# The first run-time branch of phase 2 moved ahead of the preparation of the first expert rows

## The chip, the core and the metric

The kernel runs on one core of one Trainium2 chip. A core has five engines, each with its own stream of instructions that it works off in order: TensorE (PE, matmuls), VectorE (DVE), ScalarE (ACT), GpSimd (POOL) and SyncE (SP). SP, ACT and POOL also start transfers (DMAs). Engines wait for each other by semaphores. The metric is device time in microseconds (us) for one execution.

## The reference, cut to what matters

Three stages follow one another: banded attention with 32 global tokens (4 batches, 8 heads, 512 + 32 positions, head size 64), a channel mix of width 1024, and a mixture of 8 experts, of which each of the 2176 rows uses one. Phase 2 of the kernel is the last loop of this:

```python
for b in range(B):
    prev_e = -1
    for s in range(S):
        fresh_e = int(np.argmax(logits[b, s]))
        e = fresh_e if s == 0 or local_gate[b, s] < 0.5 or prev_e < 0 else prev_e
        prev_e = e
        p = softmax(logits[b, s])
        h = np.maximum(x[b, s] @ w1[e], 0.0)      # 512 -> 1024
        out[b, s] = p[e] * (h @ w2[e])            # 1024 -> 512
```

How many rows an expert gets is known only on the chip.

## The kernel before

**Phase 1** does attention, the channel mix and the routing. A planner (`Sched`) sets its order. It leaves in HBM the mixed rows `y`, and in SBUF a list `idx` of the rows of each expert and a count `cint` of the 128-row pieces that each expert has. One piece of expert 0 is worked off already inside phase 1 (`ahead`, from L788); its result tile `oa` is sent to the output by an indirect DMA on POOL at L844.

**Phase 2** (`Experts.run`, L944) is written out by hand, and every engine works off its instructions in the order of the text. For each expert e in turn it branches on the count `cs[e]` (`first`, L932): two pieces or more go through `full` (L867, matmuls of 256 columns, tile `ph`), one piece goes through `tail` (L884, rows as the stationary operand, tile `pht`), and none leaves only the preparation of what comes next. All three sides hold the same side work, handed in as lists: `W` (conversions of the next weights) and `X` (the rows of the next expert).

**Rows.** `gather` (L852) fetches one or two pieces from `y` into a tile `xs` by indirect DMAs on POOL (L856). `prep` (L857) turns half of them: four transposes on PE into `pt` (L863), then ACT writes the high part `xh` (L865) and DVE the low part `xl` (L866). PE's first matmul of an expert needs `xh`, its third `xl`.

**Weights.** They come in parts of 512 KB into staging tiles, `st` (three, in use since phase 1) and `sw` (two, new in phase 2, in the memory that phase 1's tiles held, `oa`'s group among them). ACT makes the high part (`slot..h`, L776), DVE or POOL the low part (L779). `fetch` (L761) starts as many loads as staging tiles are free. Nearly all loads are issued by SP. Only the first two into `sw` are issued by ACT: `s.fetch(s.nc.scalar)` at L954 (the DMA itself has line L767).

**The seam between the phases** reads, in the order of the text: gathers of expert 0 (L948), reading the counts into registers of each engine (L949), `prep` of expert 0's first rows in two halves (L952), the gather for expert 1 (L953), ACT's two loads (L954), and then the loop with its first branch (L936, and L940 on the side where it is not two pieces). Each engine reads the counts and branches for itself.

The program prints both branch sides of `first` and its caller below. In the profiled execution expert 0 and expert 1 go through `tail`.

## Time and profile before

| | us |
|---|---|
| median of 3 runs (lowest, highest) | 812.99 (810.97, 813.35) |
| the profiled execution, its own time | 810.05 |
| its span | 808.3 |
| PE busy | 744.3 (92% of the span) |
| DVE, ACT, POOL busy | 523.0, 398.0, 368.3 |

The profiled execution lies 2.94 us under the median of the runs. PE is the busy engine nearly everywhere; the place of the change is one of the few where it stands still. Phase 2 begins at about 537 us of the span. Times in rows are us from the start of the span unless a column says ns; "idle before" in square brackets is how long the engine had nothing to do, and after the arrow what ended it ("issue": nothing that the profile shows as work of another).

### The profile page before, as it was taken

How to read it: one execution, taken by the hardware profiler on the slowest of the kernel's cores; microseconds unless marked ns; L12 is line 12 of the kernel's file. 1: busy time of each engine (PE TensorE's matmuls, PEld its weight loads, DVE VectorE, ACT ScalarE, POOL GpSimd, SP SyncE). 2: the span in 40 equal slices, each digit the busy share in tenths (PEclk: the TensorE clock that was granted, in tenths of full speed). 3: DMA queues.
4: the chain of work that ended last, by engine and by line, in shares of the span. 5: the costliest groups of instructions: out<-in, count | busy, mean ns of one | idle time of the engine just before them, and what ended most of it. 6: DMA issues, size and time to landing. Idle time of an engine off the chain costs nothing.

```text
span 808.3 us, 14249 instructions
## 1 busy us (share of the span) xinstructions
PE 744.3 (92%) x4790; PEld 626.2 (77%) x4790; DVE 523.0 (65%) x1482; ACT 398.0 (49%) x985; POOL 368.3 (46%) x495
## 2 busy tenths in 40 slices
PE   5987899899999999899998999987899999999974
PEld 3655687698878878888887897766697999998963
DVE  6699889776695775785766845765672725435431
ACT  4796676563555754655644432416461615224420
POOL 6678868745255462554471422134552513324130
PEclk9997899999999999899999899997999999999988
DMA  6674242211112102112102300428873523517210
GB/s 151 162 188 138 80 113 64 72 27 41 37 28 75 43 12 72 37 29 62 24 3 102 105 27 14 141 55 253 267 269 142 193 99 129 180 65 249 84 56 7
DMA packets 93966, 78.71 MB, mean 97 GB/s; under 512 B 70559, under 2 KB 74655, under 8 KB 93859
## 3 DMA queue, kind: packets, MB, share of 16 engines
q1 hardware_dynamic: 89202, 63.23, 26.2%
q0 software_dynamic: 4240, 13.11, 5.0%
q8 instruction: 54, 0.88, 0.4%
q10 hardware_dynamic: 416, 1.05, 0.4%
q14 instruction: 54, 0.43, 0.2%
HBM read 68.44 MB, written 9.70 MB: 97 GB/s over the span
## 4 chain that ended last, share of the span: by engine, by line
PE 66%; DVE 14%; DMA 10%; issue 3%; POOL 3%; ACT 2%; SPq 0%; POOLq 0%; ACTq 0%; DVEq 0%
DMA xs<-y,idx 6%; PE av L236 4%; PE psk L21 4%; PE psk L23 4%; PE psk L24 4%; PE psv L21 4%; PE psv L24 4%; PE psv L23 3%; PE ptp L228 3%; PE ph L23 3%; PE ph L24 3%; PE ph L21 3%; PE po L21 3%; PE po L23 3%; PE po L24 3%
## 5 line engine op out<-in xcount | busy, mean ns | idle before, releaser
L222 POOL TENSOR_SCALAR pl<-pl,mx 128x192 f32<-128x192 f32 (+1 forms) x128 | 66.3, 529 | 73.0 <-DVE mx L219 45.1
L21 PE MATMUL psk<-xs,slot0h 128*128 128x256 f32 x256 | 75.6, 301 | 0.9 <-ACT xs L448 0.8
L216 ACT ACTIVATE pl<-pl,mx 128x224 f32<-128x224 f32 (+1 forms) x128 | 58.8, 461 | 35.3 <-DVE mx L213 29.8
L23 PE MATMUL psk<-xs,slot0h 128*128 128x256 f32 x256 | 74.9, 293 | 0.0
L24 PE MATMUL psk<-xs,slot0l 128*128 128x256 f32 x256 | 74.9, 293 | 0.0
L856 POOL DMA_INDIRECT xs<-y,idx x32 | 38.4, 1201 | 64.3 <-PE pt L863 39.5
L922 POOL DMA_INDIRECT out_dram<-osb,idx x19 | 23.5, 1238 | 96.3 <-DVE osb L921 82.3
L450 POOL TENSOR_TENSOR xs<-xm,xs 128x512 fp32r<-128x512 f32 (+1 forms) x36 | 46.4, 1297 | 44.7 <-ACT xs L448 44.7
L877 ACT ACTIVATE hh<-ph 128x256 fp32r<-128x256 f32 x56 | 21.5, 384 | 84.1 <-PE ph L24 82.8
L443 POOL TENSOR_SCALAR xm<-xT,mut 128x256 f32<-128x256 f32 (+7 forms) x96 | 43.3, 466 | 29.6 <-DVE xT L294 16.2
L21 PE MATMUL psv<-slot1h,kh 128*128 128x512 f32 x136 | 55.0, 406 | 0.0
L23 PE MATMUL psv<-slot1l,kh 128*128 128x512 f32 x136 | 54.4, 401 | 0.3 <-POOL slot1l L417 0.3
L24 PE MATMUL psv<-slot1h,kl 128*128 128x512 f32 x136 | 54.2, 401 | 0.0
L21 PEld LDWEIGHTS psk<-xs,slot0h 128*128 128x128 f32 x256 | 49.7, 196 | 2.2 <-ACT xs L448 1.2
L23 PEld LDWEIGHTS psk<-xs,slot0h 128*128 128x128 f32 x256 | 50.5, 197 | 0.8 <-issue 0.2
L24 PEld LDWEIGHTS psk<-xs,slot0l 128*128 128x128 f32 x256 | 50.3, 197 | 0.5
L228 PE MATMUL ptp<-ident,pl 128*128 128x128 f32 x256 | 43.3, 288 | 7.6 <-DVE mxg L269 1.5
L236 PE MATMUL av<-ph,v 128*128 128x256 f32 x192 | 44.5, 292 | 2.3 <-DVE xT L294 1.0
L119 DVE TENSOR_TENSOR plo<-ptp,ph 128x512 fp32r<-128x512 f32 x48 | 32.7, 685 | 19.0 <-ACT ph L117 18.7
L878 DVE SCALAR_TENSOR_TENSOR hl<-ph,hh 128x256 fp32r<-128x256 f32 x56 | 23.7, 423 | 32.9 <-ACT hh L877 32.5
L446 DVE SCALAR_TENSOR_TENSOR xm<-xT,mut,xm 128x256 f32<-128x256 f32 (+7 forms) x96 | 41.2, 466 | 3.6 <-POOL xm L443 3.4
L228 PEld LDWEIGHTS ptp<-ident,pl 128*128 128x128 f32 x256 | 30.2, 145 | 14.7 <-POOL pl L222 4.3
(730 smaller groups left out, 2497.6 us busy)
## 6 DMA issues: line engine op xcount, KB each, us to landing
st<-in_moe_w_dram SPq DMA_DIRECT2D x42, 512.0 KB, 4.3
sw<-in_moe_w_dram SPq DMA_DIRECT2D x20, 512.0 KB, 4.4
y<-r SPq DMA_DIRECT2D x17, 256.0 KB, 2.0
qn<-in_q_l_dram SPq DMA_DIRECT2D x32, 128.0 KB, 3.0
kn<-in_k_l_dram SPq DMA_DIRECT2D x32, 128.0 KB, 2.9
earlyh<-in_moe_w_k_dram SPq DMA_DIRECT2D x8, 512.0 KB, 5.0
raw<-in_moe_w_v_dram SPq DMA_DIRECT2D x8, 512.0 KB, 3.6
vn<-in_v_l_dram SPq DMA_DIRECT2D x24, 96.0 KB, 2.1
```

What stands on the lines that cost most here:

```text
L21: i=nc.tensor.matmul(out,wh,xh,start=first,stop=False)
L23: nc.tensor.matmul(out,wh,xl,start=False,stop=False)
L24: return nc.tensor.matmul(out,wl,xh,start=False,stop=last)
L119: nc.vector.tensor_sub(out[1],x,out[0].bitcast(F32))
L216: nc.scalar.activation(p[:,h,ks],p[:,h,ks],AF.Exp,bias=mx[:,h:h+1],scale=-1.0,accum_out=mx[:,4+h:5+h])
L222: nc.gpsimd.tensor_scalar(out=p[:,h,ks],in0=p[:,h,ks],scalar1=mx[:,6+h:7+h],scalar2=0.0,op0=ALU.mult,op1=ALU.add)
L228: nc.tensor.transpose(pt[:,c,h],p[:,h,c*96:c*96+P],s.ident)
L236: nc.tensor.matmul(o,s.v(u,x,i,c),P_[y][:,c],start=c==m==0,stop=c==1 and m==len(parts)-1)
L443: nc.gpsimd.tensor_scalar(out=x[:,u,o:o+k],in0=s.xT[b][:,c,q:q+k],scalar1=m[:,1,c:c+1],scalar2=0.0,op0=ALU.mult,op1=ALU.add)
L446: nc.vector.scalar_tensor_tensor(out=x[:,u,o:o+k],in0=s.xT[b][:,c,1+q:1+q+k],scalar=m[:,0,c:c+1],in1=x[:,u,o:o+k],op0=ALU.mult,op1=ALU.add)
L450: nc.gpsimd.tensor_sub(xl[:,cs,:n],x[:,:,:n],xh[:,cs,:n].bitcast(F32))
L856: s.nc.gpsimd.indirect_dma_start(out=s.xs[i][:,j,:],out_offset=None,in_=s.y,in_offset=IndirectOffsetOnAxis(ap=s.idx[:,ch:ch+1],axis=0))
```

## The change

The two halves of `prep` and the gather for expert 1 no longer stand ahead of the loop. They become a list `rows`, handed to `first` for expert 0 alone, and run as the first thing inside the sides: all three where there are two pieces or one, and only the gather where there is none. ACT's two loads (`s.fetch(s.nc.scalar)`) stay where they were, ahead of the loop.

```diff
-    def first(s,i,i2,e,c,W,own,X):
+    def first(s,i,i2,e,c,W,own,X,rows=()):
...
         with tc.If(c>=2) as two:
-            s.full(i,e,0,list(W),[*own,*X])
+            [g() for g in rows]; s.full(i,e,0,list(W),[*own,*X])
             s.more(i2,e,1,c)
         with two.Else():
-            with tc.If(c==1) as one: again(); s.tail(i,e,0,list(W),list(X))
+            with tc.If(c==1) as one: again(); [g() for g in rows]; s.tail(i,e,0,list(W),list(X))
             with one.Else():
                 again()
-                for g in (*W,*X): g()
+                for g in (*rows[2:],*W,*X): g()
...
-        for hf in range(2): s.prep(at(0,0),0,hf)
-        s.gather(1,0)
         s.fetch(s.nc.scalar)
...
+        rows=[lambda: s.prep(at(0,0),0,0),lambda: s.prep(at(0,0),0,1),lambda: s.gather(1,0)]
         for e in range(E):
-            s.first(at(e,0),at(e,1),e,cs[e],[s.whole]*(8 if e else min(8,16-LN)) if e+1<E else (),own(e),others(e))
+            s.first(at(e,0),at(e,1),e,cs[e],[s.whole]*(8 if e else min(8,16-LN)) if e+1<E else (),own(e),others(e),() if e else rows)
```

On PE, at the seam, the order of instructions from before (minus) to the change (plus); `xs_5870` are expert 0's rows, `ph` is the first tile of the side with two pieces:

```order
 L949 TENSOR_LOAD cint
 L949 TENSOR_LOAD cmax
+L936 COMPARE_AND_BRANCH
 L863 MATMUL pt<-ident,xs_5870 128x128 x8
-L936 COMPARE_AND_BRANCH
 L21 MATMUL ph<-xh_7296,slot2h 128x256
```

The branch now stands in front of the eight transposes.

On ACT at the same place; `sw` are the two staging tiles that ACT itself loads, `xh_7296` is the high part of expert 0's rows:

```order
 L949 TENSOR_LOAD cint
 L949 TENSOR_LOAD cmax
-L865 ACTIVATE xh_7296<-pt 128x512 x2
 L767 DMA sw_7304<-in_moe_w_dram 128x1024
 L767 DMA sw_7305<-in_moe_w_dram 128x2x512
 L936 COMPARE_AND_BRANCH
+L865 ACTIVATE xh_7296<-pt 128x512 x2
 L877 ACTIVATE hh<-ph 128x256 x2
```

The two evictions have gone behind the branch, and behind the two loads too.

On ACT at the head of the side with one piece (behind L940), where `slot1h` are conversions of expert 1's weights:

```order
 L929 UNCONDITIONAL_BRANCH
 L940 COMPARE_AND_BRANCH
+L865 ACTIVATE xh_7296<-pt 128x512 x2
 L776 ACTIVATE slot1h<-st_5869 128x1024
 L776 ACTIVATE slot1h<-st_5867 128x1024
```

The evictions stand there in front of the conversions.

## Rows read from the trace of the kernel before

**Rows 1.** The page: span, and one group of DMA issues.
```profile
span 808.3 us, 14249 instructions
...
out_dram<-osb,idx POOLq DMA_INDIRECT x19, 3.6
```
**Rows 2.** Busy time of each engine (instructions), PE's granted clock, DMA share, in a stretch.
```profile
core 0: us, PE busy (x) PEld busy (x) DVE busy (x) ACT busy (x) POOL busy (x), PEclk, DMA share, GB/s
600.00:700.00 100.00, 98.88 (x615) 88.63 (x614) 49.46 (x62) 37.11 (x61) 36.38 (x25) 1.00 0.47 164
```
**Rows 3.** PE in order of time: start, us, engine, line, tiles, [idle before].
```profile
540.48 0.34 PE L681 MATMUL psL<-rt,A 128*128 128x136 f32 x2
540.87 0.30 PE L863 MATMUL pt<-ident,xs 128*128 128x128 f32 x1
542.93 0.98 PE L863 MATMUL pt<-ident,xs 128*128 128x128 f32 x7 [1.76 <-DMA xs<-y,idx]
548.74 0.77 PE L21 MATMUL pht<-slot2h,xh 128*128 128x512 f32 x1 [4.82 <-issue]
...
558.20 0.60 PE L863 MATMUL pt<-ident,xs 128*128 128x128 f32 x4
...
568.30 0.77 PE L21 MATMUL pht<-slot1h,xh 128*128 128x512 f32 x1 [3.79 <-issue]
```
**Rows 4.** ACT in order of time, its DMA issues (ACTq) among it.
```profile
543.58 1.08 ACT L865 ACTIVATE xh<-pt 128x512 fp32r<-128x512 f32 x2 [9.55 <-PE pt L863]
548.52 2.17 ACTq L767 DMA_DIRECT2D sw<-in_moe_w_dram  x2
551.03 2.95 ACT L776 ACTIVATE slot1h<-st 128x1024 fp32r<-128x1024 f32 x3 [6.37 <-issue]
...
575.05 0.60 ACT L906 ACTIVATE hs<-pht 128x512 f32<-128x512 f32 x1 [4.12 <-DMA out_dram<-osb,idx]
```
**Rows 5.** The line L844, the DMA of `oa`: issue, who waited, landing.
```profile
L844 POOL DMA_INDIRECT out_dram<-oa,idx x1: 1032/1032/1032, 542.5 to 542.5; - x1
...
  ACT slot1h L776: 6.4, 1
...
DMA to landing us min/median/max: 5.9/5.9/5.9
```
**Rows 6.** The line L767, 540 to 560 us: ns min/median/max, first and last start.
```profile
L767 ACTq EVENT_SEMAPHORE  x3: 17/38/38, 544.0 to 548.4; - x3
L767 ACTq DMA_DIRECT2D sw<-in_moe_w_dram x2: 393/1068/1743, 548.5 to 548.9; - x2
L767 SPq DMA_DIRECT2D sw<-in_moe_w_dram x2: 340/340/341, 558.3 to 559.4; - x2
```
**Rows 7.** POOL in order of time, 537 to 560 us.
```profile
542.49 1.03 POOL L844 DMA_INDIRECT out_dram<-oa,idx  x1 [0.30 <-issue]
544.08 0.98 POOL L856 DMA_INDIRECT xs<-y,idx  x1 [0.56 <-PE pt L863]
555.86 2.41 POOL L779 TENSOR_TENSOR slot1l<-sw,slot1h 128x1024 fp32r<-128x1024 f32 x1 [9.55 <-ACT slot1h L776]
```
**Rows 8.** All gathers (line L856): issue to landing.
```profile
DMA to landing us min/median/max: 3.3/5.0/7.8
```
**Rows 9.** The chain that ended last, in order of time, 535 to 552 us.
```profile
543.58 0.60 ACT xh L865
544.21 0.58 DVE xl L866
...
545.51 3.23 issue
```
**Rows 10.** Busy time by stretch again (columns as above), after PE's two longest stops.
```profile
548.74:554.62 5.88, 5.88 (x14) 4.63 (x15) 2.44 (x3) 3.34 (x4) 0.00 (x0) 0.50 0.62 191
568.30:571.70 3.40, 3.40 (x8) 2.72 (x9) 2.46 (x3) 1.06 (x1) 1.48 (x1) 0.50 1.00 351
```
**Rows 11.** What PE waited for, 540 to 809 us: total, times, longest.
```profile
PE pht L892 <- ACT hs L906: 1.8, 2, 1.5
```

## The prediction

> **What bounds the kernel now.** I read the views in this order. The page first: the reader is to see the span [rows 1], to which the profiled execution adds 1.75 us around it (810.05 us in all). [...] Then PE in order of time around the seam [rows 3]: its last matmul of phase 1 starts at 540.48, the first transpose of expert 0's rows at 540.87; the other seven wait 1.76 us for the gather, start at 542.93 and take 0.98. Then PE stands still for 4.82 us and starts expert 0 at 548.74.

> Is the 4.82 us the branch? The chain of waits says that the rows had been ready before: the first high part is started at 543.58 and takes 0.60, the first low part at 544.21, and the last 3.23 us in front of 548.74 are "issue", which is no other engine's work [rows 9]. A second such stop stands where PE goes from expert 0 to expert 1: 3.79 us [rows 3]. So a run of branches costs PE 3.8 to 4.8 us. That is what a branch moved into the wait for the gather could hide.

> Then ACT in order of time, and here is the point of the case. ACT makes the two high parts at 543.58 in 1.08 us. Its two loads are issued only at 548.52 and take until 550.69, and its next instruction starts at 551.03, after 6.37 us of idleness [rows 4]. What did ACT wait for? The line of ACT's loads shows its last semaphore wait ending at 548.4, and the first load issued 0.1 us after it [rows 6]. The line of the output DMA of tile `oa` shows who: it is issued on POOL at 542.5, lands 5.9 us later, that is at 548.4, and the trace puts ACT's 6.4 us on it [rows 5]. The `sw` tiles lie in memory that this DMA still reads. So ACT can't issue its loads before 548.4, and nothing behind them on ACT's stream starts before 551.0. Before the change the evictions stood ahead of that wait; now they stand behind it.

> **The change part by part.**

> *PE's branch moves ahead of the transposes.* It starts when PE has sent its last matmul, at 540.8 (540.48 and 0.34), and costs between 3.79 and 4.82 us as the two stops show [rows 3]: PE comes out at 544.6 to 545.6. The rows had landed by 542.93, so the eight transposes start at once and are done 1.1 us later (0.98 for seven), at 545.7 to 546.7. Their delay against before (543.91) is up to 2.8 us and is covered by what follows, as ACT is not there to take them.

> [...]

> *ACT's evictions move behind the loads and the branch.* Queue position by position: reading of the counts, load, load, branch, high part, high part. The wait for `oa`'s DMA is the one of before, and its DMA is not moved: POOL issues it at 542.49, ahead of everything that changes [rows 7]. So ACT issues the loads at 548.52, is through at 550.69, and starts its next instruction at 551.03, after the branch [rows 4]. This instruction is now the first high part, 0.60 us [rows 9], done at 551.63. PE's first matmul needs it: 551.66 with the 0.03 us that such a handover takes (543.58 + 0.60 to DVE's 544.21). The third matmul needs the low part, 551.66 + 0.58; it starts about 1 us after the first, so that is covered. **PE starts expert 0 at 551.66 and not at 548.74: a loss of 2.92 us.**

> [...] If the wait were not served on ACT, the sum would be that of the second rival.

> *Bounds of that term.* Below: `oa`'s DMA lands in 3.6 us, the median of the other output DMAs [rows 1], and not 5.9 (2.3 earlier), and the second load is issued in 0.34 us as SP does it and not in 1.743 [rows 6] (1.4 earlier); together 3.7, so -0.8 us: a small gain. It can't be much lower, as the transposes end at 545.7 at the earliest. Above: the landing takes 7.8 us, the longest of a gather [rows 8]: +1.9, so 4.8 us. I take 2.92, as its own rows give it; what is ahead of it on POOL and ACT is the same.

> *The gather for expert 1 moves behind POOL's branch,* and waits for the transposes as before. POOL's branch is not to be seen in the trace; between 0 and PE's 4.82 us. It started at 544.08 [rows 7]; now between 546 and 548.4 (543.52 + 4.82), the second issue 1.3 us later, landing at worst 7.8 us after that [rows 8], at 557.5. PE needs it at 558.20 [rows 3] plus the 2.9 of the delay. Covered, at no cost; without that cover each us would count. The two small semaphore instructions that POOL gets per gather sit in its 9.55 us of idleness in front of the low part of 555.86 [rows 7].

> *Side work of ACT and DVE.* The conversions of `slot1h` start 1.08 us later than 551.03, behind two evictions. ACT's next eviction waits for PE, which is 2.92 later, so this is covered; SP's loads into the freed tiles go out about 1.1 us later, less than PE's delay.

> *What is given back later.* Between 564 and 600 us PE's one other long wait is 1.5 us [rows 11], for an eviction that itself waits for an output DMA and starts at 575.05 [rows 4]. That DMA is issued behind work tied to PE and shifts with it; but SP's loads ahead of it in the DMA engines shift by 1.8 us less (2.92 - 1.08). Between 0 and 1.5 us; I take 0.4, near the lower end, as the loads after the first three are tied to PE again.

> *PE's clock.* [...] The stop is now longer, with eight transposes in it. [...] I take 0.

> **Sum:** 2.92 - 0.4 = +2.5 us, on the profiled execution's own 810.05, which lies 2.94 us under the median 812.99. On the median: **815.4 us**, 0.3% slower.

> **The rivals.**

> 1. *The held-up loads cost nothing* (same). ACT's second issue takes 0.34 instead of 1.743 and `oa`'s DMA lands 0.9 us earlier (less traffic behind it, since the gather for expert 1 comes later): 2.92 - 1.4 - 0.9 = +0.6, 813.6 us. For: SP never takes 1.743 us in that view. Against: what is ahead of both is unchanged. [...]

> 2. *The branch is hidden and ACT isn't held* (faster). If ACT's 6.37 us were mostly its own branch and the loads ran beside it, the evictions would follow the transposes: PE out of the branch at 544.6 to 545.6, four transposes 0.6, high part 0.6, so PE starts at 546.0 to 547.0 instead of 548.74: -1.7 to -2.7 us, 810.3 to 811.3. For: PE's stops show that the branch is dear. Against: the wait that ends at 548.4 and the load at 548.5 [rows 6]. It decides if ACT's evictions are seen before 548.

> 3. *ACT pays for its branch too.* It was there with nothing to show between 550.69 and 551.03. If it costs what PE's does, +4 us more: 819.4. Against: that same 0.34 us.

> [...]

> **How the numbers follow.** What a measurement of this kernel can tell from no change is about 0.3%, 2.4 us; the three runs lie 2.4 us apart. The forecast (+1.0 to +4.8, with rival 4) has 0.62, the first rival with the short restart 0.22, the second 0.10, the third 0.04, and 0.02 is left for others. The forecast's centre lies on the edge of 0.3%: of its 0.62, 0.36 slower and 0.26 same. The first rival is same with 0.20, and 0.02 on the faster side; the second splits 0.07 faster, 0.03 same; the third is slower. That makes faster 0.09, same 0.50, slower 0.41 with the rest. The range goes from 811.8 (the lower bound -0.8, less 0.4 for the scatter of a median of three runs) to 817.8 (the upper bound 4.8); the second and third rivals are left out.

> **What would show it.** In the profile of the changed kernel: PE's transposes of the first rows start at 544.6 to 545.6 and not at 540.87, in one piece; ACT issues its loads at about 548.5, and its first two evictions stand behind them at about 551; PE's first `pht` matmul waits for ACT's `xh` and not for "issue", at about 551.7. Wrong would be: evictions ahead of ACT's loads in time; loads issued before 547; or a first `pht` before 548.7.

## The result and the profile after

The changed kernel takes 819.5 us (median of 10 runs, 814.41 to 822.15), the kernel before in the same comparison 812.35 us (10 runs, 808.71 to 814.1). The ratio is 1.0079, with a 95% interval of 1.0058 to 1.01. The forecast was 815.4 us, its range 811.8 to 817.8: the sign was right, the time lies outside.

The page of the kernel after (span; busy time and share of PE; shares of the chain that ended last), which answers to [rows 1]:

```profile
span 820.3 us, 14250 instructions
...
PE 747.9 (91%) x4790; PEld 629.5 (77%) x4790; DVE 522.6 (64%) x1482; ACT 397.9 (49%) x985; POOL 369.4 (45%) x495
...
PE 64%; DVE 13%; DMA 12%; POOL 3%; issue 3%; ACT 3%; SPq 1%; ACTq 0%; POOLq 0%; DVEq 0%
```

The span is 12.0 us longer than before, but not all of that belongs to the change. POOL in order of time, before, the first gather of phase 2:

```profile
537.46 0.97 POOL L856 DMA_INDIRECT xs<-y,idx  x1 [19.03 <-DVE cint L699]
```

After, the first gather, the output DMA of `oa` and the gather for expert 1, beside [rows 7]:

```profile
543.87 0.97 POOL L856 DMA_INDIRECT xs<-y,idx  x1 [19.03 <-DVE cint L699]
...
548.89 1.03 POOL L844 DMA_INDIRECT out_dram<-oa,idx  x1 [0.30 <-issue]
550.49 0.98 POOL L856 DMA_INDIRECT xs<-y,idx  x1 [0.56 <-PE pt L863]
```

Phase 1 ended 6.41 us later in this one execution (822.15 us, the slowest of the ten), although its instructions are the same. In the profiles of the experiments below, whose phase 1 is the same too, the first gather lies anywhere from 535.93 to 543.05, and from 538.21 to 543.05 in those that hold the change, so I take this part for scatter. I therefore count from the first gather on: 270.8 us to the end before, 276.4 after, **5.6 us** more. That is what has to be explained.

**The seam.** PE in order of time, after, to set beside [rows 3]:

```profile
546.88 0.34 PE L681 MATMUL psL<-rt,A 128*128 128x136 f32 x2
549.26 1.06 PE L863 MATMUL pt<-ident,xs 128*128 128x128 f32 x8 [2.04 <-issue]
556.89 0.79 PE L21 MATMUL pht<-slot2h,xh 128*128 128x512 f32 x1 [6.57 <-ACT xh L865]
...
575.51 0.76 PE L21 MATMUL pht<-slot1h,xh 128*128 128x512 f32 x1 [3.88 <-ACT slot2h L776]
...
793.36 0.76 PE L21 MATMUL pht<-slot1h,xh 128*128 128x512 f32 x1 [8.16 <-issue]
```

PE's sequencer (`PEldq` in the view) at the seam, after; its branch starts 1.7 us ahead of the matmul at 546.88 (ns min/median/max, first and last start):

```profile
L936 PEldq COMPARE_BRANCH  x1: 3740/3740/3740, 545.2 to 545.2; - x1
```

The first matmul of expert 0 no longer waits for "issue" but for ACT's `xh`. ACT in order of time, after, beside [rows 4]:

```profile
555.01 0.89 ACTq L767 DMA_DIRECT2D sw<-in_moe_w_dram  x2
556.24 1.08 ACT L865 ACTIVATE xh<-pt 128x512 fp32r<-128x512 f32 x2 [15.81 <-issue]
```

The line of `oa`'s output DMA, after, beside [rows 5]:

```profile
  ACT xh L865: 15.8, 1
...
DMA to landing us min/median/max: 5.9/5.9/5.9
```

The line of ACT's loads, after (ns, first and last start), beside [rows 6]:

```profile
L767 ACTq EVENT_SEMAPHORE  x3: 38/38/2793, 545.1 to 554.9; - x3
...
L767 ACTq DMA_DIRECT2D sw<-in_moe_w_dram x2: 394/428/463, 555.0 to 555.4; - x2
```

The order is the predicted one: the DMA issued at 548.89 lands 5.9 us later, ACT's wait ends at 554.9, its loads go out, and only then come the two evictions, which PE waits for. But the loads took 0.89 us, not 2.17. From the first gather, PE starts expert 0 at 13.02 us instead of 11.28: 1.74 lost and not 2.92.

Part of it comes back at once. Busy time by stretch, after: 5.88 us from PE's restart as in [rows 10], then 7 us from the start of expert 1, then 10 us from the start of the last expert:

```profile
556.89:562.77 5.88, 5.88 (x18) 4.55 (x19) 4.78 (x5) 4.42 (x6) 0.00 (x0) 0.69 0.70 243
575.51:582.51 7.00, 6.91 (x18) 5.14 (x18) 2.87 (x3) 1.40 (x2) 1.40 (x1) 0.61 0.98 352
793.36:803.36 10.00, 10.00 (x33) 7.92 (x34) 0.69 (x1) 1.80 (x3) 0.00 (x0) 0.70 0.01 3
```

Before, PE worked the whole 5.88 us at 0.50 of its clock [rows 10]; now the mean is 0.69, that is 18 matmuls instead of 14. The granted clock is 0.50 up to 560 us and 1.00 from 561 us on, so the mean of 0.69 is 3.6 us at 0.50 and 2.2 us at 1.00; by this estimate 1.1 us are won. Expert 1 starts at 31.64 us from the first gather, before at 30.84: in this pair of profiles **the seam costs 0.8 us**, a third of the forecast. One pair is a thin measure. In the five profiles below with the seam of before (before, e0, e2, e7, e10) expert 1 starts at 29.55 to 31.18 us, 30.4 on average; in the two with the seam of after (after, e3) at 31.64 and 31.77. That makes 1.3 us.

What comes behind changes little. The same 7 us of expert 1 before:

```profile
568.30:575.30 7.00, 5.95 (x18) 4.45 (x18) 2.95 (x3) 1.30 (x2) 1.48 (x1) 0.76 1.00 363
```

Both have 18 matmuls. Before, PE was through the slow part of its restart sooner (mean clock 0.76, after 0.61) and then stood idle for 1.05 us; after, it worked slowly for 6.91 us and had no wait. A wait of 1.1 us was saved, and the slower clock took it.

**The far end.** The row at 793.36 is the surprise. Ahead of the last expert PE stands still for 8.16 us. The same row before:

```profile
782.08 0.76 PE L21 MATMUL pht<-slot1h,xh 128*128 128x512 f32 x1 [4.20 <-issue]
```

No line of the diff is near it. The lines of the branches say what PE did there. Ahead of the last expert, PE's sequencer before (ns min/median/max, first and last start):

```profile
L929 PEldq COMPARE_BRANCH  x1: 190/190/190, 778.1 to 778.1; - x1
...
L936 PEldq COMPARE_BRANCH  x1: 3399/3399/3399, 778.3 to 778.3; - x1
```

And after (the first row counts the same branch of an earlier place too, 3652 ns at 781.0):

```profile
L929 PEldq COMPARE_BRANCH  x2: 2636/3144/3652, 781.0 to 785.4; - x2
...
L936 PEldq COMPARE_BRANCH  x1: 4977/4977/4977, 788.1 to 788.1; - x1
```

One long branch (3.4 us) became two (2.6 and 5.0 us). Beside them stands one of the DMA queues, which the page calls "instruction" (54 packets and 0.88 MB in the whole execution before, so 16 KB each). Its packets during the stop (packets, MB, share of 16 engines), before (777.88 to 782.08 us) and after (785.20 to 793.36 us):

```profile
q8 instruction: 1, 0.02, 1.4%
...
q8 instruction: 3, 0.05, 3.9%
```

One packet of 16 KB became three. In the twelve profiles of this document PE has 348 branch records; 81 are longer than 2 us, and during every one of them a packet of this queue is under way. Of the 267 shorter ones, 10 have one. Chance would give it to about half of the long ones, an estimate from 27 packets in the 271 us of phase 2 in the kernel before. So a long branch goes together with a packet of this queue; what the packet brings, and whether the branch waits for it, no row shows.

The restart behind the stop differs too: before, the mean clock of the first 10 us was 0.77, with 39 matmuls,

```profile
782.08:792.08 10.00, 10.00 (x39) 8.04 (x39) 0.69 (x1) 1.79 (x3) 0.00 (x0) 0.77 0.01 3
```

and after it was 0.70 with 33 (above), another 0.7 us (10 us at 0.77 make 7.7 us of full speed, at 0.70 make 7.0). This 0.7 can't be put down to the longer stop: in the profiles below the same 10 us have 0.80 and 0.81 behind stops of 7.44 and 7.75 us (e2, e6), and 0.70 behind one of 5.02 us (e7). The whole: 0.91 us up to the last stop (240.42 to 241.33 from the first gather), 3.96 for the stop (8.16 - 4.20), 0.7 behind it: 5.6 us. The ratio of 1.0079 makes 6.4 us of 812.35, with an interval of 4.7 to 8.1.

### The profile page after: what moved, and what is told of

It reads as the page before. It is cut to its first block, busy times and chain, and to the rows that moved or that the text cites. A ratio compares the mean times of both kernels' runs of the same rounds, so it can differ in the third digit from the quotient of the medians.

```text
span 820.3 us, 14250 instructions
## 1 busy us (share of the span) xinstructions
PE 747.9 (91%) x4790; PEld 629.5 (77%) x4790; DVE 522.6 (64%) x1482; ACT 397.9 (49%) x985; POOL 369.4 (45%) x495
## 3 DMA queue, kind: packets, MB, share of 16 engines
q0 software_dynamic: 4240, 13.11, 4.9%
q10 hardware_dynamic: 416, 1.05, 0.4%
## 4 chain that ended last, share of the span: by engine, by line
PE 64%; DVE 13%; DMA 12%; POOL 3%; issue 3%; ACT 3%; SPq 1%; ACTq 0%; POOLq 0%; DVEq 0%
DMA xs<-y,idx 6%; PE av L236 4%; PE psk L21 4%; PE psv L21 4%; PE psk L23 4%; PE psv L24 4%; PE psk L24 4%; PE psv L23 3%; PE ph L23 3%; PE ph L24 3%; PE ph L21 3%; PE po L21 3%; PE po L23 3%; PE po L24 3%; PE ptp L228 3%
## 5 line engine op out<-in xcount | busy, mean ns | idle before, releaser
L856 POOL DMA_INDIRECT xs<-y,idx x32 | 38.4, 1199 | 64.2 <-PE pt L863 39.4
L228 PE MATMUL ptp<-ident,pl 128*128 128x128 f32 x256 | 45.0, 298 | 5.9 <-DVE mxg L269 1.6
L228 PEld LDWEIGHTS ptp<-ident,pl 128*128 128x128 f32 x256 | 32.0, 152 | 12.7 <-POOL pl L222 4.6
```

What stands on the lines that cost most here:

```text
L228: nc.tensor.transpose(pt[:,c,h],p[:,h,c*96:c*96+P],s.ident)
L856: s.nc.gpsimd.indirect_dma_start(out=s.xs[i][:,j,:],out_offset=None,in_=s.y,in_offset=IndirectOffsetOnAxis(ap=s.idx[:,ch:ch+1],axis=0))
```

## The experiments

**The two theories.** A: the seam alone makes the kernel slower (ACT's evictions behind its loads). B: the seam costs little, and the time is lost where PE's code further back has come to lie. The change copies the eight transposes into the sides, so that the code behind the seam begins 14 to 15 instructions later in PE's program (a count of the program; no row shows it).

For theory B the traces give this: the far stop is made of long branch records (2.6 and 5.0 us in the kernel after), and packets of the instruction queue, of 16 KB each, lie in them. Which piece of the program a packet brings is in no row here. That a shift by 256 instructions brings the stop back was my guess; e3 and e7 try it.

All profiles in one table, us; starts and ends counted from the first gather, the stop is PE's idle time ahead of the last expert. The runs e1 to e3 were compared with before at 812.06, e5 to e8 at 813.58, e9 and e10 at 813.43.

| kernel | ratio to before, 95% | first gather | expert 0 | expert 1 | last stop | end |
|---|---|---|---|---|---|---|
| before | 1 | 537.46 | 11.28 | 30.84 | 4.20 | 270.8 |
| before again (e0) | - | 538.41 | 11.18 | 30.12 | 4.22 | 270.0 |
| after | 1.0079 [1.0058, 1.01] | 543.87 | 13.02 | 31.64 | 8.16 | 276.4 |
| e1 loads late | 1.0018 [0.9984, 1.0052] | 539.15 | 7.52 | 29.32 | 7.98 | 276.1 |
| e2 before, +14 | 1.0061 [1.0027, 1.0095] | 535.93 | 11.57 | 31.18 | 7.44 | 273.2 |
| e3 after, back at 256 | 1.0025 [0.9994, 1.0057] | 538.97 | 13.11 | 31.77 | 4.94 | 273.9 |
| e5 SP loads, at 256 | 0.9963 [0.9944, 0.9982] | 539.76 | 7.14 | 28.95 | 4.96 | 269.7 |
| e6 SP loads | 1.0007 [0.998, 1.0034] | 538.21 | 7.30 | 29.38 | 7.75 | 273.4 |
| e7 before, +256 | 1.0021 [0.9997, 1.0044] | 538.04 | 11.21 | 30.41 | 5.02 | 272.4 |
| e8 before, SP loads | 0.9995 [0.9968, 1.0022] | 539.22 | 11.13 | 30.73 | 4.73 | 270.9 |
| e9 e5, `sw` behind `hh` | 0.9972 [0.9946, 0.9999] | 543.05 | 6.86 | 25.90 | 5.00 | 270.2 |
| e10 before, +128 | 0.998 [0.9952, 1.0008] | 539.61 | 11.43 | 29.55 | 5.59 | 274.9 |

Single profiles scatter: before and e0 are 0.8 us apart in the last column, and the ends of e1 and e10 lie some 4 us further out than their ratios (in e10 PE's mean clock was 0.89 from 40 to 60 us behind the first gather, in the other eleven 0.99 to 1.00). The ratios come from many runs and carry the verdicts; the profiles tell where a wait stands.

The last stop goes by the place of PE's code in all twelve: 4.20 to 4.73 us where it is not moved (before, e0, e8), 4.94 to 5.02 at 256 (e3, e5, e7, e9), 7.44 to 8.16 at 14 (after, e1, e2, e6), 5.59 at 128 (e10). Three pairs differ only in code that never runs, and their stops differ by 3.24 (e2 and before), 3.22 (after and e3) and 2.79 us (e6 and e5).

**e0: the kernel before once more**, without an edit.

> The kernel before once more, unchanged, for a second profile. Where the two profiles differ in phase 1 (first gather of phase 2 at 537.46 us before, 543.87 us in the change), this tells execution-to-execution scatter from an effect of the change. If phase 1 scatters: a first gather anywhere between 536 and 544 us. If the change slows phase 1: again within 1 us of 537.5. PE's stop in front of the last expert is 4.2 us again by every theory.

810.21 us, and the same 4.2 us at the last stop: the stop is a property of the program, not of one execution. Its first gather, at 538.41, fits both of the expectations on phase 1 and does not decide between them; the spread over all profiles does.

**e1: the evictions ahead of the loads.** In the changed kernel ACT's loads go into the sides, behind the rows.

```diff
-        s.fetch(s.nc.scalar)
...
-        rows=[lambda: s.prep(at(0,0),0,0),lambda: s.prep(at(0,0),0,1),lambda: s.gather(1,0)]
+        rows=[lambda: s.prep(at(0,0),0,0),lambda: s.prep(at(0,0),0,1),lambda: s.gather(1,0),lambda: s.fetch(s.nc.scalar)]
```

> The change, with ACT's two loads moved behind the evictions (into the sides, as last of the moved rows). Theory (the seam costs by ACT's wait, the far end by where the code lies): PE's first pht starts some 4.5 us earlier against the first gather than before (transposes at 5.4 us after the gather's issue, evictions 0.6 later), the stop in front of the last expert stays at about 8.2 us as the code on PE lies as in the change; net about 812, within 2 us of before. Rival (all of the loss is the seam and what follows it): the stop at the end is chance, 808, some 4 us faster than before.

813.91 us against 812.06. PE in order of time:

```profile
544.82 1.94 PE L863 MATMUL pt<-ident,xs 128*128 128x128 f32 x8 [2.33 <-issue]
546.67 0.79 PE L21 MATMUL pht<-slot2h,xh 128*128 128x512 f32 x1
...
554.84 1.06 PE L892 MATMUL pht<-ident,hs 128*128 128x128 f32 x4 [3.06 <-ACT hs L906]
...
788.42 0.77 PE L21 MATMUL pht<-slot1h,xh 128*128 128x512 f32 x1 [7.98 <-issue]
```

Expert 0 starts 5.5 us earlier than in the kernel after (7.52 against 13.02), with no wait at all ahead of it. The wait for `oa`'s DMA is still on ACT, though, and what now stands behind it is three conversions and `hs`: PE waits 3.06 us. Of 5.5 us, 2.3 are left at expert 1. So the order on ACT is what holds expert 0 in the kernel after, and taking it away makes the seam a gain over before at expert 1 (29.32 against 30.84). In this profile the gain is gone before the last stop, which begins at 241.29 us (240.42 before): on the way PE waits 2.36 and 1.17 us for `hs` and 0.87 for rows. The stop of 7.98 us comes on top. The time is the theory's (within 2 us of before), not the rival's 808.

**e2: only the shift.** The kernel before, and seven transposes in expert 0's side for two pieces, which this run does not take. They are never executed; they move the code behind them by 14 instructions.

```diff
+    def pad(s,n):
+        t=s.ps.tile([P,512],F32,tag="ph",name="pad",bufs=4)
+        for _ in range(n): s.nc.tensor.transpose(t[:,:P],s.ident,s.ident)
...
             s.full(i,e,0,list(W),[*own,*X])
+            if e==0: s.pad(7)
```

> The kernel before, with seven never-executed transposes at the end of expert 0's two-piece side, which moves all of PE's later code by 14 instructions as the change does (14 to 15). Nothing that runs is changed. Theory (where the code lies): PE's stop in front of the last expert goes from 4.2 to about 8 us, time +4: 816. Rival (the seam alone): no difference, 812.4, and the stop 4.2 us.

817.7 us against 812.06. PE's last stop, and PE's long branches there:

```profile
783.25 0.77 PE L21 MATMUL pht<-slot1h,xh 128*128 128x512 f32 x1 [7.44 <-issue]
```

```profile
L929 PEldq COMPARE_BRANCH  x1: 2176/2176/2176, 776.0 to 776.0; - x1
...
L939 PEldq COMPARE_BRANCH  x1: 4713/4713/4713, 778.2 to 778.2; - x1
```

Seven transposes, 14 instructions, that nobody runs cost 0.6%, and give the pair of long branches of the kernel after (L939 here is L936 there). By the ratios this is most of the result (0.61 of 0.79%), without a line of the change.

**e3: only the seam.** The changed kernel, and 121 transposes at the same place: with the change's own instructions the code behind lies 256 or 257 further than before.

```diff
+            if e==0: s.pad(121)
```

> The change, with 121 never-executed transposes at the end of expert 0's two-piece side, so that PE's later code lies 256 to 257 instructions further than before instead of 14 to 15. Nothing that runs is changed. [...] Rival (the seam alone): as the change, 819.

By theory B the stop was to go back to about 4.2 us and the seam alone to be left (0.7 to 2 us), which makes 813 to 814.5 us. Measured are 815.83 us, above that and well below the rival's 819. PE in order of time:

```profile
552.08 0.80 PE L21 MATMUL pht<-slot2h,xh 128*128 128x512 f32 x1 [6.08 <-ACT xh L865]
...
786.84 0.76 PE L21 MATMUL pht<-slot1h,xh 128*128 128x512 f32 x1 [4.94 <-issue]
```

The seam is that of the kernel after, the stop nearly that of before. The two parts, 0.61% (e2) and 0.25% (e3), make 0.86%, beside 0.79% for the change. The interval of e3 by itself touches 1, and its 0.25% (2.0 us, from -0.5 to 4.6) would also fit the 2.5 us of the forecast. The profiles don't settle it: expert 1 starts 0.9 us later than before, as in the kernel after, but the last stop begins 2.5 us later (242.93 against 240.42; after: 0.91), as PE waits 1.19 us for rows and 0.97 for `hs` on the way. So the seam costs 0.8 to 2.5 us, with the forecast at the upper end.

**e7 and e10: the shift by itself, in two more sizes.** The kernel before with 128 and with 64 transposes (256 and 128 instructions). If the place decides, I expected no change from e7 (812 us within 1.5, a stop of 4.2 us), and from e10 one of the two kinds of stop seen till then: 4.2 to 5.0 us and a time of 813, or 7.4 to 8.2 us and 817.

> [...] Rival (never-executed code costs by being there, or by any shift): 816 to 818, as with seven.

> The kernel before with 64 transposes that never run at the end of expert 0's two-piece side: PE's code behind the seam lies 128 instructions further (14 made the stop ahead of the last expert 7.4 us and the time 1.006 of before; 256 made the stop 5.0 us and the time 1.002). The seam itself is unchanged. [...] Rival (what counts is how far the code is moved, whatever the place): between the runs of 14 and 256 instructions, a stop near 6.2 us, 815.5 us.

e7: 814.04 us against 813.58, and the stop is 5.02 us: 18 times the shift of e2, and a third of its cost, with 1 in the interval. How far the code moves is not what counts. Nor is it the tile that the transposes write, which takes a turn of the `ph` buffers: e7 and e10 have it too, and the kernel after, e1 and e6 have the long stop without it. e10 missed both of its forecasts: 812.33 us against 813.43, no slower than before, with a stop of 5.59 us. Its branches show a third pattern. All of PE's L930 and L929 from 600 to 800 us, before:

```profile
L930 PEldq COMPARE_BRANCH  x8: 64/296/5140, 605.2 to 750.9; - x8
...
L929 PEldq COMPARE_BRANCH  x6: 64/64/3297, 605.1 to 778.1; - x6
```

and in e10:

```profile
L930 PEldq COMPARE_BRANCH  x8: 64/284/1361, 610.1 to 755.9; - x8
...
L929 PEldq COMPARE_BRANCH  x6: 64/64/396, 609.9 to 783.1; - x6
```

The long ones (5.1 and 3.3 us) are gone from both lines; they cost little, as PE still had matmuls to work off under them (under the one of 5140 ns, from 605.25 us on, matmuls start up to 608.95 us, and the stop behind them was 1.10 us). In front of the last expert L929 takes 0.4 us and the branch of `first` (L936 in before, L939 here) 4.6. So the place decides which branches are long, but my "two kinds of stop" was too simple, and there is no rule here that gives a stop from a place.

**e6, e5, e8: the wait taken off ACT.** SP issues the two loads, so that ACT waits for nothing ahead of its evictions. e6 is the changed kernel with that, e5 has the 121 transposes of e3 as well, e8 is the kernel before with that.

```diff
-        s.fetch(s.nc.scalar)
+        s.fetch()
```

> The same with SP's loads, without the never-executed transposes: the code lies as in the change. Theory: the seam as in the run with them, the stop in front of the last expert about 8 us, so 3 to 4 us slower than that run: 812. Rival (the place of the code does nothing): equal to that run.

> The change, with the first two loads issued by SP instead of ACT, and with 121 never-executed transposes that put PE's later code 256 to 257 instructions further than before. Theory (ACT's hold-up at the seam and the place of the code are the two costs): no hold-up, PE's first pht at about 7.2 us after the first gather (11.2 before, 13.0 in the change), expert 1 starts at about 27 (30.5 before), the stop in front of the last expert 4 to 5 us as before: some 3.5 us faster than before, 808.5. Rival (the gain is eaten by the next wait, as when the loads stood behind the evictions and PE waited 3.1 us for hs): 811.

> The kernel before with the first two loads issued by SP instead of ACT, nothing else. Theory: PE at the seam is bound by its branch (4.8 us), the evictions stood ahead of the loads anyway; only ACT's conversions start earlier (about 546 instead of 551): same, 812 to 811. Rival (ACT's hold-up costs in the kernel before too): 2 to 4 us faster.

e5 takes 810.91 us against 813.58 and is **faster than before**; e6, which differs by the shift alone, takes 814.26, and its stop is 7.75 us; e8 takes 811.99, no difference. In time e5 lies nearer to its rival (811) than to its theory (808.5): the waits below eat part of the gain. PE in e5:

```profile
545.24 1.34 PE L863 MATMUL pt<-ident,xs 128*128 128x128 f32 x8 [2.12 <-issue]
546.90 0.50 PE L21 MATMUL pht<-slot2h,xh 128*128 128x512 f32 x1 [0.33 <-ACT xh L865]
...
557.09 0.50 PE L21 MATMUL po<-slot0h,hh 128*128 128x512 f32 x1 [2.94 <-ACT hh L894]
568.71 0.62 PE L21 MATMUL pht<-slot1h,xh 128*128 128x512 f32 x1 [2.60 <-ACT slot2h L776]
```

This is what the change was able to do: the branch lies under the wait for the gather, and PE goes from the transposes to expert 0 in 0.33 us. In e8 PE still starts at 11.13, as in the kernel before: loads on SP are worth nothing without the branch moved, and the branch moved is no gain with the loads ahead of the evictions on ACT (e3). In e5 the wait is now for `hh`, because ACT stands at the conversion ahead of it. ACT in e5:

```profile
555.49 1.06 ACT L776 ACTIVATE slot1h<-sw 128x1024 fp32r<-128x1024 f32 x1 [3.47 <-DMA sw<-in_moe_w_dram]
556.46 0.58 ACT L894 ACTIVATE hh<-pht 128x512 fp32r<-128x512 f32 x1
```

**e9: that conversion behind `hh`,** in e5.

```diff
-            if b==0: go(W,TW[0])
+            if b==0 and e: go(W,TW[0])
```

> The changed kernel with the loads of the first rows on SP's queue and the code behind the seam moved by 121 transposes that never run, as in the run of 810.9 us, and one edit more: for expert 0 the conversion of the weights of the own column (sw) goes behind the eviction hh instead of ahead of it, since in that run PE waited 2.94 us for hh while ACT waited for sw's DMA. Theory (ACT's place in line costs what PE waits): PE's wait for hh goes, expert 1 starts 26.0 to 26.8 us behind the first gather (28.95 there), 808 us. Rival (the wait moves): hs, which needs sw, becomes late instead; PE waits for hs about as long, expert 1 starts at 28.5 to 29, 811 us.

811.25 us against 813.43: not the 808 of my theory. PE's waits in e9 (us in total, times, longest):

```profile
PE pht L21 <- issue: 6.3, 3, 5.0
PE pht L892 <- ACT hs L906: 5.3, 2, 4.3
PE pht L21 <- ACT slot3h L776: 3.4, 1, 3.4
```

The wait for `hh` is gone and expert 1 starts at 25.90, 3.1 us earlier than in e5, as the theory said. But then PE waits 4.30 us for expert 1's `hs` (in e5 1.80), and the next matmuls start at 36.16 from the first gather, in e5 at 36.72. ACT in e9:

```profile
567.03 1.06 ACT L776 ACTIVATE slot3h<-st 128x1024 fp32r<-128x1024 f32 x1 [1.70 <-DMA st<-in_moe_w_dram]
...
571.64 1.06 ACT L776 ACTIVATE slot2h<-sw 128x1024 fp32r<-128x1024 f32 x1 [1.97 <-DMA sw<-in_moe_w_dram]
574.66 1.06 ACT L776 ACTIVATE slot2h<-st 128x1024 fp32r<-128x1024 f32 x1 [1.96 <-DMA st<-in_moe_w_dram]
578.56 0.60 ACT L906 ACTIVATE hs<-pht 128x512 f32<-128x512 f32 x1 [2.84 <-DMA out_dram<-osb,idx]
```

The conversions wait for their loads one after the other, and `hs` then waits 2.84 us more for expert 0's output DMA: `hs` and the output tile take turns in the same two buffers (`osb`), and that DMA is issued only at 570.71, behind POOL's low part of `slot3`. So transfers, of weights and of that output, now set the pace of the first two experts, and not the place of one conversion; that is the rival, a wait that moves. No run here tells whether fewer other transfers at the seam would speed them up, or a third buffer.

## Why the prediction was wrong

- **PE's branch ahead of the transposes: right, but for its start.** PE's sequencer branches at 545.2 for 3.74 us (5.31 before) while the engine waits for the gather anyway; the transposes start in one piece 5.39 us from the first gather, before 5.47 (the last seven). The text let the branch start when PE had sent its last matmul, and had the transposes wait 1.7 to 2.7 us for it; the record starts 1.7 us ahead of that matmul (545.2 against 546.88), and they did not wait.
- **The evictions behind the wait, the loads and the branch: right in every step of the queue.** Wait, landing of 5.9 us, loads, 0.34 us, evictions, PE. The term was mis-sized: 1.74 instead of 2.92 us, since the second load was issued in 0.46 us and not in 1.743. That goes with the order of the instructions more than with chance: the second issue took 1.42 to 1.74 us in four of the five profiles with the seam of before (0.57 in e2), and 0.45 to 0.52 in the three that hold the change with loads on ACT (after, e1, e3). Why is not shown. The lower bound of the term named just this saving (1.4).
- **PE's clock: taken as 0, 1.1 us won** at the first restart. No run shows the 0; the profiles have a mean clock of 0.69 over 5.88 us after, 0.50 before, and the 1.1 is the estimate from these. It made the seam's cost 0.8 us in this pair. Part of it is scatter: the first 10 us of expert 0 have a mean clock of 0.71 in before, 0.79 in e0, 0.77 in e7, and 0.82 in after and e3.
- **Given back later: 0.4 taken.** The place was right: expert 1's wait for `hs` went from 1.5 to 0.4 us. But PE's slower restart at expert 1 took the same again, so that nothing was given back; PE was 0.7 us late behind that wait and 0.9 at the last stop.
- **The sum: the step that failed.** It ended at the seam: what PE loses there, less 0.4, was taken as the loss at the end. That the loss goes on holds in the profile of the kernel after (0.8 us at expert 1, 0.9 at 240 us; in e3 0.9 and 2.5), but the sum had no term for code that the diff does not touch and only moves. That was 3.96 us at the last stop (8.16 instead of 4.20); e2 lost 0.61% by it without the change. With the seam alone the time would have been 813.8 (the profile's 0.8) to 815.0 (e3's ratio), inside the range. The prediction had before it that branches cost PE 3.8 to 4.8 us; it did not ask what the eight transposes, written into two sides instead of one place ahead of them, do to all the branches behind. That the sign came out right is in the larger part luck: the seam's own share, 0.25% in e3, is not clear of noise.
- **Rivals.** 1, the cheap second issue, with the short restart of the clock that its 0.22 takes in, comes nearest to what the seam did (0.8 us; it said 0.6), but without the earlier landing of `oa`'s DMA, which took 5.9 us again. 2 failed by ACT's wait, at 554.9. 3 failed: ACT's branch takes 0.05 us (L936, 50 ns). A second stop of PE at the seam, which the forecast's 0.62 takes in as rival 4, did not come: there is one long branch record there (3740 ns), and L940 behind it takes 78 ns. The text's word that POOL's branch is not to be seen was wrong; the view of L936 has it in the kernel before, 53 ns at 544.4.
- **The gather for expert 1 and the side work: right,** at no cost; the gather stands 6.62 us from the first one, as before (544.08 - 537.46, 550.49 - 543.87).

What stays open: by what rule a place of the code gives a stop of 4.2, 5.0, 5.6 or 7.4 us, one packet of the instruction queue in it or three, and why e2's ratio (5.0 us) is larger than its stop's 3.2 us; the interval of the ratio (2.2 to 7.7 us) allows both.

## What to carry to other kernels

Before work is moved behind a wait, read which instructions of the same engine stand there: here two evictions of 0.6 us each, put behind two loads that wait for a DMA, cost PE 1.7 us at expert 0, and the change starts expert 0 4.1 us earlier than before once another engine issues the loads; that is a gain (0.9963) if the code behind lies as in e5, and none (1.0007) if it lies as in the change. In a kernel with run-time branches, an edit's cost is not only at its place: compare the stops at all later branches (here 8.16 us instead of 4.20 ahead of the last expert), and test a shift by instructions that never run (here 14 of them cost 0.61%) before a difference of half a per cent is put down to the edit. When a stop is removed, the next limit (here the loads of the weights and an output's transfer) may lie close behind it: 4 us won at expert 0 were 2 us at expert 1 and 0.4% at the end.
